# A fused attention and gated-MLP kernel whose prologue gets a new order: value tiles loaded ahead of the second weight chunk, sums of values ahead of the turns of pairs 1 and 3

## Chip, cores and metric

The kernel runs on one core of one Trainium2 chip. The metric is device microseconds of one execution; below, "us" is always that. The time before is the median of three executions.

## The reference, cut to what matters

```python
# attention: q, k, v are (4 batches, 8 heads, 768 positions, 64)
k_sum = k.reshape(B, H, 24, 32, D).max(axis=3)     # pooled keys
v_sum = v.reshape(B, H, 24, 32, D).mean(axis=3)    # pooled values
scores_l = scale * q @ k.T, kept where |i - j| < 16 (else -1e9)
scores_s = scale * q @ k_sum.T + log(32)
a = softmax(concat([scores_l, scores_s]))          # max, exp, sum, divide by sum + 1e-9
x = a @ concat([v, v_sum])                         # to 3072 tokens x 512
# MLP, weights given in float64: 512 -> 1536 -> 512
g = x @ w_gate
out = (g * sigmoid(g) * (x @ w_val)) @ w_out
```

## The kernel before, in words

The 3072 tokens are worked in six blocks of 512. The eight heads are four pairs (pair u holds heads 2u and 2u+1). The hidden width of 1536 is worked in twelve chunks j of 128. An MLP chunk is twelve products for `gate`, twelve for `val` and twelve for `down` on TensorE, each 128x128 by 128x512: every operand is split into a high and a low part, and high x high, high x low and low x high are summed, which gives the three products per 128x128 tile.

Block 0 and the weights are the prologue. Attention of block 0 goes pair by pair. `kf`, `qf` and `kq` load keys and queries. `pool(u)` takes the pooled maximum of the keys on VectorE, `sw(0,u)` and `sp(0,u)` are the score products with the window and with the pooled keys. `ttr0` and `ttr1` (four VectorE operations each, one half, that is one head of the pair, each) add the bias and take the row maximum, `exp0` and `exp1` (four ScalarE operations each) take exponentials and row sums, `rcp` inverts the sums, and `nrm` multiplies. `tr0` and `tr1` turn a half on TensorE (four 128x128 transposes), `pt0` and `pt1` copy it out of PSUM. `fv` is the matrix product that sums the values over blocks of 32, `fvc` copies the sums out. `out` and `outp` multiply the turned weights with the values (window and pooled), `split` and `rest` make the high and low part of x. `ve`, `vo` and `vr` load the three parts of the value tile.

Weights arrive as the two 32-bit halves of float64. `w_load` loads a chunk; `w_abs` (ScalarE), `w_c1`, `w_c2`, `w_s1`, `w_s2` (VectorE) rebuild float32 by integer operations, `w_hi` and `w_lo` split it into high and low part. "g", "v" and "o" are the three weights; "gv" is gate and value together, twice as wide. `silu`, `mul`, `ah` and `al` make the split activation for `down`. Steps `load`, `keys`, `scores`, `load_values`, `pool_values` and `values` belong to attention of block 1, which runs in the prologue between the chunks of block 0.

The order of the prologue is written out by hand as the text `PROLOGUE`, some 450 steps. Each step issues its instructions at once, and line 848 makes every instruction follow the one before it on the same engine. So each engine works through its own list in the order of the text, and an engine waits where its next step has an input missing, with all that stands behind it. DMAs are all issued by SyncE, in the same order. A mark behind a step picks the engine (`=a` ScalarE, `=d` VectorE, `=p` GpSimd) or the PSUM bank group (`y`, `g`: two banks each, `c`: four). A number behind a bank letter puts filler products in front of the step: `zeros` multiplies a tile of zeros, one unit for each 128 columns, with a result that is overwritten. `WARM` issues seven units at the very start.

Buffers rotate: pools `psg` and `psy` have two banks, `psc` four, tiles `a`, `ah` and `al` two buffers each, and `dec` three. `room(0)` closes the pool of block 0's attention tiles and opens the later ones in its place, so that loads behind it wait for block 0's attention to end. From block 1 on a fixed loop issues `gate`, `val` and `down` of each chunk, with attention of later blocks between them.

Of the kernel before, what the change touches and what calls it, by code (L numbers as in the profile page):

```python
# [110 lines left out]
room(0) rest(0,1) gate(0,0,0) split(0,2)=a gate(0,0,1) rest(0,2) gate(0,0,2) split(0,3)=a rest(0,3) w_c1(2,gv)
w_abs(3,gv) gate(0,0,3) gate(0,1) silu(0,0) w_c1(3,gv) w_c2(2,gv) w_s2(0,o) w_lo(0,v)=p w_s1(2,gv) w_c2(3,gv)
w_s2(2,gv) w_abs(1,o) val(0,0,0) val(0,0,1) silu(0,1) w_hi(0,o)=a val(0,0,2) w_s1(3,gv) w_c1(1,o) val(0,0,3)
load(1,0) val(0,1) w_hi(2,gv)=a w_lo(2,gv)=d w_load(2,o) w_c2(1,o) mul(0,0) ah(0,0)=a keys(1,0) gate(0,2)
w_abs(2,o) mul(0,1) w_lo(0,o)=d w_s1(1,o) al(0,0)=d ah(0,1)=a w_s2(3,gv) w_load(3,o) w_load(4,gv) silu(0,2)
scores(1,0) down(0,0) val(0,2) w_s2(1,o) w_hi(3,gv)=a al(0,1)=d ttr0(1,0) pool_values(1,0) ttr1(1,0)
w_lo(3,gv)=p w_abs(4,gv) w_abs(3,o) w_c1(4,gv) w_c1(2,o) w_c2(4,gv) gate(0,3) mul(0,2) val(0,3) w_load(5,gv)
w_s1(4,gv) w_c1(3,o) w_s2(4,gv) exp1(1,0) w_hi(1,o)=a w_c2(3,o) w_lo(1,o)=d exp0(1,0) w_hi(4,gv)=a w_s1(3,o)
w_c2(2,o) w_s2(3,o) w_s1(2,o) w_load(7,gv) w_load(6,gv) rcp(1,0) down(0,1) w_lo(4,gv)=d load(1,1) silu(0,3)
w_abs(5,gv) w_hi(3,o)=a w_c1(5,gv) mul(0,3) gate(0,4) val(0,4) ah(0,2)=a w_abs(7,gv) w_c2(5,gv) w_lo(3,o)=d  # L120
w_s1(5,gv) w_s2(2,o) nrm(1,0)=a w_hi(2,o)=a w_s2(5,gv) al(0,2)=d w_hi(5,gv)=a tr0(1,0) silu(0,4) w_abs(6,gv)
w_load(4,o) tr1(1,0) pt0(1,0)=a w_abs(4,o) w_lo(2,o)=d pt1(1,0)=a down(0,2) keys(1,1) mul(0,4) w_c1(6,gv)
w_lo(5,gv)=d w_c1(4,o) scores(1,1) ah(0,4)=a w_c2(6,gv) ah(0,3)=a ttr0(1,1) exp0(1,1) ttr1(1,1) al(0,4)=d
w_load(5,o) load_values(1,0) w_load(7,o) w_load(6,o) w_c1(7,gv) w_s1(6,gv) values(1,0)=a w_load(9,gv) gate(0,5)
al(0,3)=p w_abs(5,o) w_c2(4,o) w_s2(6,gv) w_load(8,gv) w_s1(4,o) val(0,5) w_c2(7,gv) w_hi(6,gv)=a down(0,3)
out(1,0) silu(0,5) w_lo(6,gv)=d w_s2(4,o) w_c1(5,o) w_s1(7,gv) gate(0,6) w_abs(6,o) mul(0,5) w_hi(4,o)=a
w_lo(4,o)=p down(0,4) pool_values(1,1) w_s2(7,gv) w_c2(5,o) load_values(1,1) exp1(1,1) w_c1(6,o) w_s1(5,o)
w_abs(7,o) w_abs(9,gv) w_c1(9,gv) w_c1(7,o) val(0,6) w_hi(7,gv)=a w_lo(7,gv)=d w_c2(9,gv) split(1,0)=a w_s2(5,o)
rcp(1,1) silu(0,6) w_abs(8,gv) w_c2(6,o) w_s1(9,gv) load(1,2) mul(0,6) rest(1,0) w_hi(5,o)=a w_c2(7,o) ah(0,5)=a
values(1,1)=a al(0,5)=p w_load(8,o) w_load(10,gv) w_s1(6,o) gate(0,7) silu(0,7) nrm(1,1)=a w_load(9,o) val(0,7)  # L130
w_c1(8,gv) w_lo(5,o)=d w_s2(9,gv) w_hi(9,gv)=a tr0(1,1) down(0,5) mul(0,7) ah(0,7)=a pt0(1,1)=a keys(1,2)
scores(1,2) pool_values(1,2) tr1(1,1) w_lo(9,gv)=d w_s2(6,o) w_abs(8,o) w_s1(7,o) gate(0,9) ttr0(1,2) ttr1(1,2)
pt1(1,1)=a w_c2(8,gv) out(1,1) ah(0,6)=a load(1,3) w_hi(6,o)=a w_lo(6,o)=d exp0(1,2) al(0,6)=p w_s2(7,o)
w_c1(8,o) exp1(1,2) w_hi(7,o)=a w_s1(8,gv) al(0,7)=d w_s2(8,gv) w_c2(8,o) val(0,9) down(0,6) w_lo(7,o)=d
w_abs(10,gv) w_abs(9,o) w_c1(9,o) w_hi(8,gv)=a w_c1(10,gv) w_lo(8,gv)=d down(0,7) silu(0,9) rcp(1,2) w_c2(10,gv)
w_s1(10,gv) mul(0,9) split(1,1)=a w_s2(10,gv) w_c2(9,o) nrm(1,2)=a gate(0,8) tr0(1,2) w_hi(10,gv)=a keys(1,3)
w_lo(10,gv)=d w_s1(8,o) val(0,8) ah(0,9)=a rest(1,1) room(1) w_load(11,v) w_load(11,g) silu(0,8) mul(0,8)
load_values(1,2) w_load(10,o) w_load(11,o) w_s2(8,o) pt0(1,2)=a al(0,9)=p w_abs(11,v) ah(0,8)=a w_hi(8,o)=a
w_s1(9,o) al(0,8)=d w_lo(8,o)=d gate(0,10) w_c1(11,v) tr1(1,2) pt1(1,2)=a w_c2(11,v) w_s2(9,o) w_s1(11,v)
w_s2(11,v) scores(1,3) ttr0(1,3) values(1,2)=a w_hi(9,o)=a silu(0,10) down(0,8) ttr1(1,3) val(0,10) w_abs(11,g)  # L140
w_c1(11,g) w_c2(11,g) w_lo(9,o)=p out(1,2) w_s1(11,g) w_s2(11,g) w_abs(10,o) exp1(1,3) w_hi(11,g)=d w_c1(10,o)
w_hi(11,v)=a down(0,9) w_lo(11,g)=p exp0(1,3) split(1,2)=d mul(0,10) w_lo(11,v)=d w_c2(10,o) rcp(1,3) ah(0,10)=a
rest(1,2) gate(0,11) w_abs(11,o) w_c1(11,o) w_c2(11,o) load_values(1,3) nrm(1,3)=a w_s1(10,o) tr0(1,3)
pt0(1,3)=a w_s2(10,o) al(0,10)=d w_hi(10,o)=a silu(0,11) pool_values(1,3) val(0,11) tr1(1,3) pt1(1,3)=a
values(1,3)=a w_s1(11,o) w_lo(10,o)=d down(0,10) w_s2(11,o) out(1,3) w_hi(11,o)=d w_lo(11,o)=p mul(0,11)
# [799 lines left out]
```

## Time and profile before

| what | value |
|---|---|
| time, median of 3 executions | 674.53 us (674.5 to 674.58) |
| the profiled execution's own time | 674.72 us |
| its span, first to last instruction | 673.0 us |
| TensorE matmul busy | 667.7 us, 99% of the span |
| VectorE, ScalarE, GpSimd busy | 340.0, 297.3, 139.6 us |
| share of the chain that ended last | TensorE 97%, VectorE 2% |

The span leaves out 1.7 us that lie before the first and after the last profiled instruction. A busy TensorE means that a matmul was in flight. The chain that ended last is followed back from the last instruction, at each step to what released it or to the instruction before it on its engine.

### The profile page before, as it was taken

To read this page: it belongs to the slowest core of one execution; us is meant where nothing else is said; L and a number is where in the kernel's file an instruction comes from. 1 tells how busy PE (TensorE), PEld (TensorE's weight loads), DVE (VectorE), ACT (ScalarE), POOL (GpSimd) and SP (SyncE) were. 2 spreads that over 40 slices of the span, in tenths; PEclk is the share of its full clock that TensorE was granted. 3 is DMA by queue.
4 is the path that set the end of the run, shared out by engine and by line. 5 is a ranking of instruction groups with operands and counts; after the bars stand their busy time and mean duration, and the time that the engine had idled before them with its cause. 6 is when DMAs were issued, how large, how long until landed. Compare 5 with 4: busy or idle time off the path is not lost.

```text
span 673.0 us, 12398 instructions
## 1 busy us (share of the span) xinstructions
PE 667.7 (99%) x4936; PEld 544.0 (81%) x4936; DVE 340.0 (51%) x952; ACT 297.3 (44%) x729; POOL 139.6 (21%) x137
## 2 busy tenths in 40 slices
...
GB/s 336 336 379 345 42 238 171 47 120 135 56 58 0 56 45 122 95 10 79 103 2 168 57 49 82 17 39 65 56 57 57 0 25 0 63 1 0 1 0 64
DMA packets 72059, 60.19 MB, mean 89 GB/s; under 512 B 42272, under 2 KB 60064, under 8 KB 70464
## 3 DMA queue, kind: packets, MB, share of 16 engines
...
q14 instruction: 20, 0.16, 0.1%
...
## 4 chain that ended last, share of the span: by engine, by line
PE 97%; DVE 2%; issue 0%; DVEq 0%
PE g L647 30%; PE v L647 29%; PE acc L694 29%; PE xo L612 4%; PE sc L447 2%; DVE p L505 1%; PE pp L563 1%; PE sc L458 1%; PE xo L620 1%; PE warm L740 0%; DVE ks L336 0%; PE pv L415 0%; PE sc L472 0%; PE end L694 0%; DVE m_g L219 0%
## 5 line engine op out<-in xcount | busy, mean ns | idle before, releaser
L694 PE MATMUL acc<-w_o,ah 128*128 128x512 f32 x572 | 176.2, 389 | 0.0
L647 PE MATMUL g<-xh,w_gv 128*128 128x512 f32 x480 | 159.7, 394 | 0.0
L647 PE MATMUL v<-xh,w_gv 128*128 128x512 f32 x480 | 157.9, 390 | 0.0
L658 DVE TENSOR_TENSOR a<-v,a 128x512 f32<-128x512 f32 x72 | 49.6, 689 | 199.5 <-PE v L647 197.9
L178 POOL TENSOR_TENSOR al<-a,ah 128x512 fp32r<-128x512 f32 x63 | 81.8, 1299 | 328.1 <-ACT ah L182 328.1
L694 PEld LDWEIGHTS acc<-w_o,ah 128*128 128x128 f32 x572 | 107.4, 188 | 22.2
L182 ACT CAST ah<-a 128x512 fp32r<-128x512 f32 x71 | 44.0, 621 | 168.5 <-DVE a L658 168.5
L694 PE MATMUL acc<-w_o,al 128*128 128x512 f32 x286 | 112.0, 392 | 0.0
L647 PEld LDWEIGHTS g<-xh,w_gv 128*128 128x128 f32 x480 | 90.1, 188 | 20.8 <-ACT w_o L182 0.2
L647 PEld LDWEIGHTS v<-xh,w_gv 128*128 128x128 f32 x480 | 90.1, 188 | 18.9
L653 ACT ACTIVATE a<-g 128x512 f32<-128x512 f32 x72 | 43.1, 599 | 134.8 <-PE g L647 131.8
L647 PE MATMUL g<-xl,w_gv 128*128 128x512 f32 x240 | 93.8, 391 | 0.0
L593 DVE STREAM_TRANSPOSE pt_short<-p_short 32x256 f32<-32x256 f32 x192 | 83.8, 436 | 19.8 <-POOL p_short L548 16.9
L647 PE MATMUL v<-xl,w_gv 128*128 128x512 f32 x240 | 93.4, 389 | 0.0
L694 PEld LDWEIGHTS acc<-w_o,al 128*128 128x128 f32 x286 | 53.7, 188 | 11.4 <-DVE al L178 0.2
L647 PEld LDWEIGHTS v<-xl,w_gv 128*128 128x128 f32 x240 | 45.1, 188 | 9.3
L647 PEld LDWEIGHTS g<-xl,w_gv 128*128 128x128 f32 x240 | 45.1, 188 | 8.8
L521 ACT ACTIVATE p_short<-p_short,nm 128x88 f32<-128x88 f32 x128 | 45.3, 355 | 0.2
L178 DVE TENSOR_TENSOR xl<-xo,xh 128x512 fp32r<-128x512 f32 x24 | 16.4, 686 | 56.9 <-ACT xh L182 56.8
L548 POOL TENSOR_TENSOR p_short<-p_short,ri 128x704 f32<-128x704 f32 x16 | 26.0, 1623 | 53.5 <-DVE ri L539 49.6
L647 PE MATMUL g<-xh,w_g 128*128 128x512 f32 x96 | 32.2, 396 | 0.0
L647 PE MATMUL v<-xh,w_v 128*128 128x512 f32 x96 | 31.6, 390 | 0.0
...
## 6 DMA issues: line engine op xcount, KB each, us to landing
raw_gv<-in_wgv SPq DMA_DIRECT2D x10, 1024.0 KB, 11.6
...
```

The source lines that it names most:

```text
L178: (nc.vector if e == "d" else nc.gpsimd).tensor_tensor(out=out, in0=a, in1=b.bitcast(F32), op=ALU.subtract)
L182: nc.scalar.copy(out, in_)
L447: nc.tensor.matmul(sc[h][s * SQ : (s + 1) * SQ, c * SC : (c + 1) * SC], t["q"][hs, i * SQ : (i + 1) * SQ], keys[hs], start=True, stop=True,)
L458: nc.tensor.matmul(sc[h][s * QT : (s + 1) * QT, c * KC : (c + 1) * KC], t["q"][hs, qs], t["kw"][hs, i, :], start=True, stop=True,)
L521: nc.scalar.activation(out=t["p"][:, i, :kc], in_=t["p"][:, i, :kc], func=AF.Exp, scale=-1.0, bias=t["nm"][:, i : i + 1], accum_out=t["sm" ...
L548: (nc.vector if on == "d" else nc.gpsimd).tensor_tensor(out=p, in0=p, in1=ri.rearrange("p (n o) -> p n o", o=1).broadcast_to([P, 2 * NTP, ...
L593: nc.vector.transpose(out=to[r * SQ : (r + 1) * SQ, :, s * SQ : (s + 1) * SQ], in_=t["p"][s * SQ : (s + 1) * SQ, :, at : at + SQ],)
L612: nc.tensor.matmul(ps[hs, qs], vw, t["pt"][:n, h, qs], start=k not in OWN or i == 0, stop=k not in OWN)
L647: nc.tensor.matmul(ps, w[:, cs], x, start=u == 0 and n == 0, stop=u == NP - 1 and n == 2)
L653: nc.scalar.activation(out=a, in_=A.pop(("g", k, j)), func=AF.Silu)
L658: nc.vector.tensor_tensor(out=a, in0=ps, in1=a, op=ALU.mult)
L694: nc.tensor.matmul(out, a[:, ts], w[:, cs], start=begin and n == 0, stop=end and n == 2)
```

## The change

The text of the prologue is replaced. It has the same 457 steps as before; their order, some engine marks, some bank letters and the filler numbers differ. Four places in the code change with it: the 24 columns of lead space go to chunk 11's gate weight in place of its value weight; `sp` may have filler units of its own (no step in the new text asks for any); `a_max` allocates a pair's tiles at whichever half comes first; `m_down` opens the accumulators at whichever chunk comes first.

The core of the diff, with the part of the order up to the first MLP chunk and the first steps behind it:

```diff
-kf(2) qf(2) qf(0) sw(0,2)=cc pool(2) sp(0,2) kf(0) ttr0(0,2) pool(0) exp0(0,2) ttr1(0,2) exp1(0,2)
-sw(0,0)=yg2 sp(0,0) kq(1) kq(3) ttr0(0,0) pool(1) rcp(0,2) nrm(0,2)=p ttr1(0,0) exp0(0,0) w_load(0,g)
-sw(0,1)=yg6 sp(0,1) w_load(1,gv) vr() ve() exp1(0,0) ttr0(0,1) vo() tr0(0,2)=c9 ttr1(0,1) rcp(0,0) w_abs(0,g)
-exp1(0,1) w_c1(0,g) pool(3) exp0(0,1) w_c2(0,g) w_s1(0,g) w_abs(1,gv) rcp(0,1) tr1(0,2)=g sw(0,3)=cy4 sp(0,3)
-ttr0(0,3) nrm(0,0)=p tr0(0,0)=c3 ttr1(0,3) exp0(0,3) exp1(0,3) pt0(0,2)=a w_s2(0,g) w_c1(1,gv) w_c2(1,gv)
-rcp(0,3) tr1(0,0)=y nrm(0,1)=p tr0(0,1)=y1 w_s1(1,gv) tr1(0,1)=c nrm(0,3)=d w_s2(1,gv) fv()=g pt1(0,2)=a
-w_load(0,v) out(0,2)=c pt0(0,0)=a fvc()=a outp(0,2) pt1(0,0)=a out(0,0)=c tr0(0,3)=c pt0(0,1)=a w_load(0,o)
...
+kf(2) qf(2) qf(0) sw(0,2)=cc pool(2) sp(0,2) kf(0) ttr0(0,2) exp0(0,2) ttr1(0,2) pool(0) exp1(0,2) sw(0,0)=yg5
+sp(0,0) kq(1) kq(3) ttr0(0,0) pool(1) rcp(0,2) nrm(0,2)=p ttr1(0,0) exp0(0,0) w_load(0,g) sw(0,1)=yg3 sp(0,1)
+vr() ve() exp1(0,0) ttr0(0,1) w_load(0,v) vo() w_load(1,gv) ttr1(0,1) rcp(0,0) nrm(0,0)=p pool(3) w_abs(0,g)
+sw(0,3)=cy3 sp(0,3) tr0(0,2)=c exp0(0,1) ttr1(0,3) tr1(0,2)=c w_c1(0,g) exp1(0,1) tr1(0,0)=y tr0(0,0)=y
+exp1(0,3) w_load(1,o) rcp(0,1) w_c2(0,g) ttr0(0,3) pt1(0,0)=d pt0(0,0)=a fv()=g w_abs(0,v) w_c1(0,v) pt0(0,2)=a
+w_s1(0,g) exp0(0,3) w_load(0,o) pt1(0,2)=a nrm(0,1)=p w_c2(0,v) w_s2(0,g) w_load(2,gv) rcp(0,3) fvc()=a
+w_s1(0,v) w_hi(0,g)=a cst() w_abs(1,gv) nrm(0,3)=d tr1(0,1)=c out(0,2)=y6 outp(0,2) w_s2(0,v) tr0(0,1)=c
+w_abs(1,o) tr0(0,3)=c w_lo(0,g)=d w_c1(1,gv) w_c1(1,o) tr1(0,3)=c pt0(0,1)=a out(0,0)=y w_c2(1,gv) pt1(0,3)=a
+pt0(0,3)=a w_c2(1,o) w_load(2,o) w_s1(1,gv) outp(0,0) pt1(0,1)=a out(0,1)=g w_abs(0,o) w_s1(1,o) w_s2(1,gv)
+w_c1(0,o) outp(0,1) split(0,0)=a w_abs(2,gv) split(0,2)=a out(0,3)=c outp(0,3) rest(0,0) split(0,1)=a
+w_hi(0,v)=a split(0,3)=a w_c1(2,gv) w_lo(0,v)=p rest(0,1) rest(0,2) rest(0,3) w_hi(1,gv)=a gate(0,0,0)
+w_lo(1,gv)=d gate(0,0,1) w_c2(2,gv) room(0) gate(0,0,2) w_load(3,gv) gate(0,0,3) gate(0,1) w_c2(0,o) load(1,0)
+w_s1(2,gv) w_abs(3,gv) val(0,1) val(0,0,0) w_s1(0,o) val(0,0,1) w_s2(2,gv) silu(0,0) w_c1(3,gv) keys(1,0)
+w_hi(2,gv)=a w_load(4,gv) w_load(8,o) silu(0,1) scores(1,0) val(0,0,2) w_s2(1,o) mul(0,1) w_s2(0,o)
+load_values(1,0) w_load(5,gv) w_hi(1,o)=a w_abs(4,gv) w_abs(2,o) ah(0,1)=a val(0,0,3) w_lo(2,gv)=d w_c2(3,gv)
+w_load(3,o) ttr1(1,0) mul(0,0) w_hi(0,o)=a gate(0,2) ttr0(1,0) val(0,2) exp1(1,0) w_s1(3,gv) al(0,1)=p
+w_lo(1,o)=d w_s2(3,gv) w_abs(5,gv) w_c1(5,gv) exp0(1,0) rcp(1,0) w_c1(4,gv) w_hi(3,gv)=a w_lo(3,gv)=d
+pool_values(1,0) load(1,1) down(0,1) w_lo(0,o)=p ah(0,0)=a w_load(5,o) silu(0,2) mul(0,2) gate(0,3) w_load(4,o)
...
     def w_lead(j, nm):
-        return LEAD if (nm, j) == ("v", NJ - 1) else 0
+        return LEAD if (nm, j) == ("g", NJ - 1) else 0
...
     def a_far(k, u):
+        for _ in range(int(on) if on.isdigit() else 0):
+            nc.tensor.matmul(t["sc"][0][:, NTP * KC :], warm[:, :P], warm[:, : TOK - NTP * KC], start=True, stop=True)
...
     def a_max(k, u, g):
-        if g == 0 and k >= SHORT:
+        first = "p" not in t
+        if first and k >= SHORT:
...
     def m_down(k, j):
-        if j == 0:
+        first = k not in ACC
+        if first:
```

## Rows read from the trace of the kernel before

**Rows 1.** The page: busy us, share of the span, instructions.

```profile
PE 667.7 (99%) x4936; PEld 544.0 (81%) x4936; DVE 340.0 (51%) x952; ACT 297.3 (44%) x729; POOL 139.6 (21%) x137
```

**Rows 2.** Waits of TensorE, whole span, all there are: total us, times, longest.

```profile
PE warm L740 <- DVE warm L816: 1.5, 1, 1.5
PE pp L740 <- DVE nm L505: 0.3, 1, 0.3
PE sc L484 <- DVE ks L336: 0.2, 1, 0.2
```

**Rows 3.** Windows: us, busy of PE, PEld, DVE, ACT, POOL, clock, DMA share, GB/s.

```profile
46.00:100.00 54.00, 54.00 (x356) 43.88 (x345) 53.24 (x109) 49.35 (x101) 7.60 (x8) 1.00 0.65 225
...
670.00:673.00 3.00, 0.00 (x0) 0.00 (x0) 0.32 (x1) 0.00 (x0) 0.00 (x0) 1.00 0.51 179
```

**Rows 4.** The chain that ended last: start us, us, what.

```profile
43.04 2.72 PE g L647 x12
...
46.74 2.99 PE acc L694 x12
```

**Rows 5.** Timeline of SyncE's issues: start us, us, DMA.

```profile
6.24 0.57 SPq L797 DMA_DIRECT2D vrows<-in_vO  x1
```

**Rows 6.** DMA issues to 60 us: KB each, median us to landing.

```profile
vrows<-in_vO SPq DMA_DIRECT2D x1, 1024.0 KB, 15.9
```

**Rows 7.** Timeline of TensorE: start us, us, instruction, count, idle before and releaser.

```profile
9.24 0.66 PE L484 MATMUL sc<-ks,kq 64*64 64x24 f32 x32 [0.21 <-DVE ks L336]
...
12.57 2.21 PE L740 MATMUL pp<-warm 128*128 128x512 f32 x6
14.62 1.04 PE L563 MATMUL pp<-consts,p 128*120 128x128 f32 x8
...
22.91 1.15 PE L612 MATMUL xo<-pt,vrows 96*64 96x64 f32 x32
...
25.96 0.65 PE L563 MATMUL pp<-consts,p 128*120 128x128 f32 x4
...
31.87 0.50 PE L647 MATMUL g<-xh,w_g 128*128 128x512 f32 x1
```

**Rows 8.** Timeline of VectorE, to 46 us.

```profile
7.42 0.28 DVE L505 CUSTOM_DVE_ANT_0 p<-sc,bias 128x120 f32<-128x120 f32 x1 [2.31 <-PE sc L484]
...
8.24 0.95 DVE L336 TENSOR_REDUCE ks<-kq 128x24 f32<-128x768 f32 x1
...
11.64 0.16 DVE L538 TENSOR_SCALAR sm<-sm 128x8 f32<-128x8 f32 x1
...
11.95 0.23 DVE L505 CUSTOM_DVE_ANT_0 p<-sc,bias 128x120 f32<-128x120 f32 x1
...
15.87 1.15 DVE L219 TENSOR_SCALAR m_g<-m_g 128x512 int32<-128x512 int32 x1
...
35.46 0.68 DVE L234 SCALAR_TENSOR_TENSOR m_o<-raw_o,m_o 128x512 int32<-128x512 int32 x1
36.06 1.22 DVE L227 SCALAR_TENSOR_TENSOR m_gv<-raw_gv,m_gv 128x1024 int32<-128x1024 int32 x1
37.20 0.68 DVE L219 TENSOR_SCALAR m_gv<-m_gv 128x1024 int32<-128x1024 int32 x1
```

**Rows 9.** Timeline of ScalarE, to 50 us.

```profile
10.95 0.38 ACT L521 ACTIVATE p<-p,nm 128x120 f32<-128x120 f32 x1
...
12.46 0.38 ACT L521 ACTIVATE p<-p,nm 128x120 f32<-128x120 f32 x1
...
13.97 0.66 ACT L210 ACTIVATE m_g<-raw_g 128x512 f32<-128x512 f32 x1
...
21.61 1.53 ACT L182 COPY pt<-pp 120x512 f32<-120x512 f32 x3
...
27.36 1.05 ACT L182 CAST w_gv<-m_gv 128x1024 fp32r<-128x1024 f32 x1
```

**Rows 10.** Timeline of GpSimd, to 50 us.

```profile
14.89 1.85 POOL L548 TENSOR_TENSOR p<-p,ri 128x960 f32<-128x960 f32 x1 [0.91 <-DVE ri L539]
```

More of the change, by code (lines that the diff above doesn't have):

```diff
@@ L106 @@
-rcp(0,3) tr1(0,0)=y nrm(0,1)=p tr0(0,1)=y1 w_s1(1,gv) tr1(0,1)=c nrm(0,3)=d w_s2(1,gv) fv()=g pt1(0,2)=a
-w_load(0,v) out(0,2)=c pt0(0,0)=a fvc()=a outp(0,2) pt1(0,0)=a out(0,0)=c tr0(0,3)=c pt0(0,1)=a w_load(0,o)
-w_abs(0,v) pt1(0,1)=a w_c1(0,v) w_hi(0,g)=a w_c2(0,v) w_abs(0,o) outp(0,0) tr1(0,3)=y w_lo(0,g)=d w_hi(1,gv)=a
-w_s1(0,v) w_load(2,gv) w_c1(0,o) w_s2(0,v) w_load(3,gv) w_lo(1,gv)=d w_c2(0,o) out(0,1)=y split(0,0)=a rest(0,0)
-w_s1(0,o) pt0(0,3)=a pt1(0,3)=a outp(0,1) w_abs(2,gv) split(0,1)=a w_load(1,o) cst() w_hi(0,v)=a out(0,3)=g outp(0,3)
@@ L111 @@
[L111 to L145, printed above, removed]
@@ L146 @@
-ah(0,11)=d al(0,11)=d split(1,3)=a down(0,11) rest(1,3) load(2,0)
+kf(2) qf(2) qf(0) sw(0,2)=cc pool(2) sp(0,2) kf(0) ttr0(0,2) exp0(0,2) ttr1(0,2) pool(0) exp1(0,2) sw(0,0)=yg5
+sp(0,0) kq(1) kq(3) ttr0(0,0) pool(1) rcp(0,2) nrm(0,2)=p ttr1(0,0) exp0(0,0) w_load(0,g) sw(0,1)=yg3 sp(0,1)
+vr() ve() exp1(0,0) ttr0(0,1) w_load(0,v) vo() w_load(1,gv) ttr1(0,1) rcp(0,0) nrm(0,0)=p pool(3) w_abs(0,g)
+sw(0,3)=cy3 sp(0,3) tr0(0,2)=c exp0(0,1) ttr1(0,3) tr1(0,2)=c w_c1(0,g) exp1(0,1) tr1(0,0)=y tr0(0,0)=y
@@ new lines @@
+load_values(1,0) w_load(5,gv) w_hi(1,o)=a w_abs(4,gv) w_abs(2,o) ah(0,1)=a val(0,0,3) w_lo(2,gv)=d w_c2(3,gv)
+w_load(3,o) ttr1(1,0) mul(0,0) w_hi(0,o)=a gate(0,2) ttr0(1,0) val(0,2) exp1(1,0) w_s1(3,gv) al(0,1)=p
+w_lo(1,o)=d w_s2(3,gv) w_abs(5,gv) w_c1(5,gv) exp0(1,0) rcp(1,0) w_c1(4,gv) w_hi(3,gv)=a w_lo(3,gv)=d
+pool_values(1,0) load(1,1) down(0,1) w_lo(0,o)=p ah(0,0)=a w_load(5,o) silu(0,2) mul(0,2) gate(0,3) w_load(4,o)
+nrm(1,0)=a w_c1(2,o) w_c2(4,gv) al(0,0)=p w_c2(2,o) w_abs(3,o) w_s1(4,gv) w_load(6,gv) w_s1(2,o) tr0(1,0)
@@ new lines @@
+w_c2(5,gv) w_load(7,gv) values(1,0)=a silu(0,3) keys(1,1) w_c1(3,o) w_s2(4,gv) w_load(7,o) pt0(1,0)=a
+w_load(9,o) val(0,3) w_s2(2,o) tr1(1,0) pt1(1,0)=a w_s1(5,gv) w_hi(4,gv)=a w_lo(4,gv)=d scores(1,1) ttr1(1,1)
+out(1,0) ah(0,2)=a w_hi(2,o)=a w_abs(6,gv) mul(0,3) w_abs(4,o) w_load(6,o) w_c2(3,o) w_s2(5,gv) w_s1(3,o)
+split(1,0)=a w_c1(4,o) w_c1(6,gv) w_hi(5,gv)=a down(0,0) w_s2(3,o) w_abs(7,gv) w_load(10,gv) al(0,2)=d gate(0,4)
+val(0,4) w_lo(2,o)=p silu(0,4) w_c2(6,gv) w_load(9,gv) w_lo(5,gv)=d w_s1(6,gv) pool_values(1,1) w_hi(3,o)=a
@@ new lines @@
+ttr0(1,1) mul(0,4) ah(0,3)=a down(0,2) exp1(1,1) w_s2(6,gv) w_c1(7,gv) gate(0,5) w_abs(5,o) ah(0,4)=a w_c2(4,o)
+w_abs(6,o) w_c2(7,gv) silu(0,5) w_hi(6,gv)=a al(0,3)=p val(0,5) w_abs(9,gv) w_s1(4,o) w_c1(5,o) w_lo(3,o)=p
+down(0,3) w_c2(5,o) w_s2(4,o) w_lo(6,gv)=d rest(1,0) al(0,4)=d w_hi(4,o)=a w_load(8,gv) exp0(1,1) w_s1(7,gv)
+mul(0,5) gate(0,6) w_lo(4,o)=d w_s1(5,o) ah(0,5)=a w_s2(7,gv) load_values(1,1) w_abs(8,gv) w_c1(9,gv) w_c1(8,gv)
+val(0,6) w_c1(6,o) rcp(1,1) w_hi(7,gv)=a w_lo(7,gv)=d down(0,4) w_c2(6,o) w_s2(5,o) silu(0,6) gate(0,7)
@@ new lines @@
+nrm(1,1)=a load(1,2) keys(1,2) w_c2(9,gv) w_hi(5,o)=a mul(0,6) tr0(1,1) values(1,1)=a pt0(1,1)=a al(0,5)=d
+w_s1(6,o) val(0,7) w_s1(9,gv) tr1(1,1) w_c2(8,gv) w_s2(9,gv) w_lo(5,o)=d scores(1,2) silu(0,7) w_s2(6,o)
+w_s1(8,gv) w_abs(9,o) pt1(1,1)=a mul(0,7) pool_values(1,2) w_hi(9,gv)=a out(1,1) down(0,5) ttr1(1,2) ttr0(1,2)
+w_s2(8,gv) w_load(10,o) load(1,3) w_lo(9,gv)=p ah(0,6)=a w_hi(6,o)=a w_lo(6,o)=d al(0,6)=d split(1,1)=d
+w_abs(7,o) w_abs(10,gv) w_c1(10,gv) gate(0,9) val(0,9) exp0(1,2) w_hi(8,gv)=a w_c1(9,o) w_c2(10,gv) ah(0,7)=a
@@ new lines @@
+w_c1(7,o) exp1(1,2) w_s1(10,gv) down(0,6) w_lo(8,gv)=d silu(0,9) gate(0,8) w_abs(8,o) val(0,8) rest(1,1)
+w_s2(10,gv) rcp(1,2) mul(0,9) w_hi(10,gv)=a nrm(1,2)=a load_values(1,2) tr1(1,2) al(0,7)=d silu(0,8) w_c2(7,o)
+ah(0,9)=a w_c1(8,o) w_c2(9,o) values(1,2)=a w_lo(10,gv)=d w_s1(9,o) room(1) keys(1,3) gate(0,10) w_s1(7,o)
+w_load(11,g) w_load(11,v) mul(0,8) w_s2(9,o) tr0(1,2) w_s2(7,o) w_hi(9,o)=d pt1(1,2)=a scores(1,3) w_c2(8,o)
+w_lo(9,o)=d pt0(1,2)=a out(1,2) al(0,9)=d w_abs(11,g) w_s1(8,o) silu(0,10) w_abs(11,v) load_values(1,3)
```

13 lines of the change are left out of this document (10 added, 3 removed).

## Prediction

> **What bounds the kernel.** I read the page first, then TensorE's waits, the windows, the chain that ended last, and last the four engines' lists in order of time up to the first MLP product.
>
> The page has TensorE busy for 667.7 us of a span of 673.0 [rows 1]. Its list of waits has three entries, 2.0 us in all, and the last in time is a turn's filler that waits for a row maximum of pair 3 [rows 2]. From there to the last product TensorE never stands still for as long as the list counts, and the chain that ended last runs through TensorE alone; twelve 512-wide products take 2.72 us [rows 4]. So the reader is to see two stretches. Before the first MLP product, at 31.87 us [rows 7], TensorE works on what VectorE and ScalarE give it, with fillers in between. Behind it lies one block of products, which the change reorders inside block 0 but doesn't shorten: the new text has the same steps. The end can thus move only by when the first MLP product starts, by holes in the block behind it, and by the clock, which was 1.00 [rows 3].
>
> The profiled execution took 674.72 us for its span of 673.0; its median is 674.53. I add my differences to the median.
>
> **The change, part by part.** *Code.* The lead space, the filler loop in `sp` (no step asks for it) and the two `first` flags issue no instruction: nothing.
>
> *Loads.* The values' second part landed at 6.24 + 15.9 = 22.1 us [rows 5, 6], and the first product that reads it began at 22.91 [rows 7]. It was queued behind 1024 KB of chunk 1's weights, and now behind 512 KB of chunk 0's value weight instead. By its own size and the 2.7 us that it took in this queue (an estimate: 1024 KB at some 400 GB/s), it lands 1.3 us earlier, at 20.8. Chunk 1's weights land some 7 us later, at 23; ScalarE doesn't come to them before 24.9 in the walk below, so that is free. It would cost as much as they are late beyond that.
>
> *Fillers.* Units fall from 25 to 17 (5, 3, 3 and 6). Nine took 14.62 - 12.57 = 2.05 us [rows 7], so eight are 1.8 us of TensorE. That is a gain only where TensorE's own list is the limit. The walk says it isn't, so I take 0, and keep 1.8 for the range.
>
> *Start of the order.* Up to the first row maximum at 7.42 [rows 8] nothing differs. Four maxima take 0.82 and a pooled maximum 0.87, its result after 0.95 [rows 8]. Both halves of pair 2 now come ahead of `pool(0)`: it starts at 7.42 + 1.63 = 9.05 and is done at 10.00, against 9.19. Pair 0's far scores wait for it and take 0.66 [rows 7]; their maxima start at 10.75, where before the far scores were in time. Then VectorE does 0.82 of maxima, 0.87 of `pool(1)`, 0.31 of inverse (11.64 to 11.95) [rows 8], and reaches pair 0's second half at 12.75. ScalarE gets its first value 0.3 later, at 13.05; before, that half started at 12.46 [rows 9]. From here ScalarE has something to do all the time, and its list up to pair 2's second copy is: four exponentials, the absolute value of chunk 0, twelve exponentials, a copy, an absolute value, a copy, four exponentials. Four exponentials take 12.46 - 10.95 = 1.51, an absolute value of 512 some 0.57 (0.66 less about 0.09 by which neighbours overlap, as the three copies do), a copy 0.51 [rows 9]: 5 x 1.51 + 2 x 0.57 + 2 x 0.51 = 9.71. The copy starts at 22.76 and ends at 23.34, and `out(0,2)` follows at 23.4 in place of 22.91.
>
> What hides the rest: `pool(3)` comes late (about 15.5 to 16.4), so TensorE stands still for some 2 us ahead of pair 3's far scores, but pair 3's maxima are still ready at 17.2, before ScalarE asks for them at 18.2. The sums of values now run at about 18.8 to 20.6, on data that is queued ahead of the values' second part. TensorE's list reaches `out(0,2)` at about 22.3, fillers and all, and waits 1.1 there.
>
> From `out(0,2)` to the first MLP product it was 31.87 - 22.91 = 8.96 with two turns among it. Now three turns are left, 0.44 more at most (a turn of four shows 0.65, some 0.2 of it tail) [rows 7]; they stand together and save a switch of shape. I take 0.2 (bounds 0 and 0.44): the first MLP product at 23.4 + 9.2 = 32.6, that is 0.7 later.
>
> *Behind the first product.* Chunk 1's gate comes second, and its low part is made last. ScalarE must split pair 3 (0.5), then cast chunk 1 (1.05) [rows 9], and VectorE subtracts: VectorE begins that 1.7 after the first product. From there its list runs without a gap through nine wide or integer steps to pair 1's first maxima of block 1, which free a bank for `gate(0,2)`: four wide steps at 1.14, three at 0.60, four of 512 at 0.60, the pooled keys at 0.87, an integer step of 0.3, four maxima at 0.82 [rows 8]: 1.7 + 4.56 + 1.80 + 2.40 + 0.87 + 0.30 + 0.82 = 12.45, and 0.2 for latencies. TensorE is there after 46.74 - 2.72 - 31.87 = 12.15 plus the 0.27 that a change from scores to products costs [rows 4]: 12.42. A hole of 0.25. Lower bound 0, upper bound what a VectorE 2% slower would add, 0.5.
>
> *The rest of block 0.* VectorE was busy 53.24 of 54 us there [rows 3], so cover is thin. Up to the first product it idles about 1.3 us more than before (0.8 for pair 0's scores, 0.8 for pair 3's, against some 0.3 in the same places), which the 0.7 of later start repays half: 0.6 us of its work moves behind. The margins along the new lists are some tenths; I take 0 and bound it by 0.6, and by 0.85 more for overlap of GpSimd with VectorE.
>
> That overlap has a row: a 512-wide integer step took 1.15 us at 15.87 where half of a 1024-wide one takes 0.3 [rows 8]; it ended 0.3 after GpSimd's multiply, which ran from 14.89 to 16.74 [rows 10]. The 0.85 is that loss, once. The new order gives GpSimd eight low parts in place of six. The Trainium skill ("SBUF — State Buffer", section "Who interferes with whom") says that VectorE and GpSimd share a port pair as an exclusive lock and whichever starts later waits for all of the other's instruction. The row agrees. By that rule one or two more VectorE steps would wait and the sum would be up to 0.85 higher; without it the sum stays.
>
> Sum: 0.7 + 0.25 = 0.95; 674.53 + 0.95 = 675.5 us.
>
> **The rivals.** *TensorE's list is the limit, and fillers removed are time saved.* Then the eight units go off the end: 674.53 - 1.8 = 672.7. For it: TensorE shows only 0.5 us of idle behind its first product [rows 2], and values land earlier. Against it: fillers stand where TensorE would wait anyway, and ScalarE's 9.71 us don't shrink. It decides if the second copy of pair 2 is done before 21.5.
>
> *The gain and the loss meet.* Later scores are made good, for instance by ScalarE waiting less than I think; 674.5.
>
> *Buffers are handed out in turn.* `silu(0,2)` stands ahead of `al(0,0)` and behind `al(0,1)`. If its buffer is the one that is free, no wait; if it is the older, it waits for GpSimd's low part, and the same order comes again at chunks 7 to 9. One such wait is 1.3 us and four or five make 6: 681. In the old order both rules give the same, so no row decides.
>
> *VectorE falls behind.* The 0.6 and 0.85 above, both in full: 675.5 + 1.45 = 676.95.
>
> *The clock falls in the new hole.* Some 2 us at 14.4 to 16.4 with almost nothing on TensorE. If it drops to 1.2 GHz, some 5.9 us of work ahead of `out(0,2)` (far scores, turns, sums, fillers; an estimate) take up to 11.8: +4.8 if it stays low, some 2.4 if it returns half way, 677.9. Against: at the end, 3.0 us without a product left the clock at 1.00 [rows 3]. The Trainium skill ("TensorE: Matmul & The Clock Gate", section "Part 1: The HAM clock gate (the "warmup" mystery)") says that the half clock is the default and activity lifts it, so fewer fillers count against this change; that row shows a longer hole passed without a drop.
>
> **How the numbers follow.** Forecast 0.61 (own range 674.6 to 676.6), TensorE's list 0.12, gain and loss meet 0.08, VectorE behind 0.08, buffers in turn 0.06, clock 0.05. A measurement of this kernel tells about 0.2%, 1.35 us, from no change: 673.2 to 675.9. Of the forecast 0.40 lies within and 0.21 above. Faster 0.12, same 0.48, slower 0.40. The range, 673.0 to 678.0, leaves out the first rival's core and the buffers.
>
> **What would show it.** Right: first MLP product at 32.3 to 32.8, just ahead of it a wait of about 1 us of `out(0,2)` for ScalarE's copy, a wait of about 2 us of pair 3's far scores for VectorE, the values landed by 21, and holes below 0.6 us in all behind it. Wrong: a first product before 31.5; a wait of a `gate` for a `silu` that itself waits for GpSimd; a granted clock under 1.00; or holes behind 46 us.

## The result: 679.99 us, 0.86% slower, and the profile after

The changed kernel takes 679.99 us (median of four, 679.74 to 681.54) against 674.51 of the kernel before on the same chip: ratio of the mean times 1.0086, 95% interval 1.0068 to 1.0103. The profiled execution took 679.74 us, with a span of 678.0 against 673.0 [rows 1]. The number of a line (L650) is up to four higher in the changed kernel than before; in the experiments, whose order wraps differently, it is two lower again.

TensorE's longest waits, which answer to [rows 2]: engine, what waited, for what; then us in total, times, the longest.

```profile
PE g L650 <- ACT a L656: 1.6, 1, 1.6
PE warm L744 <- DVE warm L820: 1.5, 1, 1.5
PE sc L486 <- DVE ks L336: 1.3, 3, 0.8
PE v L650 <- DVE w_v L178: 1.3, 1, 1.3
PE sc L458 <- POOL kw L184: 1.2, 1, 1.2
```

Three waits of over a microsecond are new, each happens once, and each has another releaser: ScalarE's silu, a low part by VectorE, and a copy by GpSimd. The windows say where they lie (stretch, then busy time of TensorE, its weight loads, VectorE, ScalarE and GpSimd, granted clock, DMA share, GB/s); they answer to [rows 3].

```profile
33.00:46.00 13.00, 12.83 (x83) 9.74 (x82) 12.87 (x31) 9.41 (x12) 2.41 (x5) 1.00 0.99 288
46.00:60.00 14.00, 12.42 (x57) 9.96 (x56) 12.83 (x20) 12.91 (x36) 3.15 (x4) 1.00 0.72 256
60.00:80.00 20.00, 18.81 (x139) 15.38 (x138) 19.82 (x42) 14.71 (x26) 8.60 (x5) 1.00 1.03 377
...
120.00:145.00 25.00, 23.71 (x165) 19.29 (x163) 23.20 (x53) 18.52 (x45) 6.22 (x6) 1.00 0.12 38
145.00:400.00 255.00, 255.00 (x1987) 209.47 (x1987) 124.08 (x390) 98.93 (x258) 58.46 (x53) 1.00 0.29 76
```

TensorE is short of 1.58, 1.19 and 1.29 us in three of them and full again from 145 on, at a granted clock of 1.00 throughout. TensorE's list in order of time gives the four instants that matter (start, duration, in brackets the idle time before it).

```profile
31.90 0.50 PE L650 MATMUL g<-xh,w_g 128*128 128x512 f32 x1
...
54.76 0.50 PE L650 MATMUL g<-xh,w_gv 128*128 128x512 f32 x1 [1.58 <-ACT a L656]
...
63.29 0.64 PE L458 MATMUL sc<-kw,q 64*64 64x120 f32 x16 [1.19 <-POOL kw L184]
...
138.90 0.50 PE L650 MATMUL v<-xh,w_v 128*128 128x512 f32 x1 [1.29 <-DVE w_v L178]
```

The first MLP product is where it was: 31.90 against 31.87 [rows 7]. So in this execution nothing was won or lost in front of it, and nearly the whole loss lies in the three holes. Start to start they cost 1.75 us (`gate(0,3)` begins at 54.76, `down(0,1)` began at 50.29 and needs 2.72), 1.34 (the second half of `scores(1,1)` at 63.29, the first at 61.45, a half needs 0.5) and 1.35 (`val(0,11)` at 138.90, the turns ahead of it at 137.02 need 0.53): 4.4 of the 5.0 us. (The expectations below count the first two from the last product that began ahead of them, and say 1.97 and 1.45.) Of the rest, 0.2 lies at `gate(0,1)` (34.95, behind 34.53, where a product needs 0.23) and 0.3 at `gate(0,2)` (44.75, behind 44.22).

**Hole 1, ScalarE's list.** ScalarE from the arrival of chunk 4's weights to the silu that frees the bank of `gate(0,3)`, then VectorE, then GpSimd:

```profile
42.21 1.19 ACT L210 ACTIVATE m_gv<-raw_gv 128x1024 f32<-128x1024 f32 x1 [0.87 <-DMA raw_gv<-in_wgv]
...
45.02 1.28 ACT L524 ACT_TABLE_LOAD   x1
...
48.68 1.16 ACT L210 ACTIVATE m_gv<-raw_gv 128x1024 f32<-128x1024 f32 x1 [0.74 <-DMA raw_gv<-in_wgv]
...
52.81 1.28 ACT L656 ACT_TABLE_LOAD   x1
54.11 0.60 ACT L656 ACTIVATE a<-g 128x512 f32<-128x512 f32 x1
```

```profile
46.06 2.12 DVE L227 SCALAR_TENSOR_TENSOR m_gv<-raw_gv,m_gv 128x1024 int32<-128x1024 int32 x1
```

```profile
45.80 1.30 POOL L178 TENSOR_TENSOR w_o<-m_o,w_o 128x512 fp32r<-128x512 f32 x1
...
52.87 1.79 POOL L178 TENSOR_TENSOR al<-a,ah 128x512 fp32r<-128x512 f32 x1 [5.76 <-ACT ah L182]
```

`silu(0,2)` could run from about 47.7, when `gate(0,2)` ends, but stands behind the exponentials of block 1, two table loads, and the casts and absolute values of later weights; from 42.21 to 54.11 ScalarE rests only for late weights. The VectorE step at 46.06 took 2.12 where the same form takes 1.22 elsewhere: it ended only after GpSimd's residue of the output weights. These 0.9 us didn't reach TensorE: ScalarE's next cast of a weight (51.23) waited for nothing, and VectorE itself stood 0.80 us for ScalarE's exponentials at 51.37.

**Hole 2, a copy by GpSimd.** GpSimd, and VectorE beside it:

```profile
59.96 3.27 POOL L184 COPY kw<-ks 128x96 f32<-128x96 f32 x1 [5.09 <-DVE ks L336]
```

```profile
59.82 0.42 DVE L215 TENSOR_SCALAR m_o<-m_o 128x512 f32<-128x512 f32 x1
60.15 1.22 DVE L234 SCALAR_TENSOR_TENSOR m_gv<-raw_gv,m_gv 128x1024 int32<-128x1024 int32 x1
61.29 0.68 DVE L234 SCALAR_TENSOR_TENSOR m_o<-raw_o,m_o 128x512 int32<-128x512 int32 x1
61.89 1.22 DVE L227 SCALAR_TENSOR_TENSOR m_gv<-raw_gv,m_gv 128x1024 int32<-128x1024 int32 x1
63.25 1.23 DVE L178 TENSOR_TENSOR w_gv<-m_gv,w_gv 128x1024 fp32r<-128x1024 f32 x1
```

The copy of the pooled keys takes 0.26 us alone, here 3.27. It ends at 63.23, in the first gap that VectorE leaves, 63.11 to 63.25, and TensorE's scores wait for it. Steps with two inputs in SBUF that follow one another don't always do this. A later copy of the kernel before was held for one of them only, although the next one followed at once and itself took 0.75 in place of 0.68:

```profile
114.66 1.27 POOL L184 COPY kw<-ks 128x96 f32<-128x96 f32 x1 [12.50 <-DVE ks L336]
```

```profile
114.57 1.23 DVE L178 TENSOR_TENSOR w_gv<-m_gv,w_gv 128x1024 fp32r<-128x1024 f32 x1
115.71 0.75 DVE L227 SCALAR_TENSOR_TENSOR m_o<-raw_o,m_o 128x512 int32<-128x512 int32 x1
```

Why it is three steps in one place and one in the other stays open.

**Hole 3, a low part by VectorE.** GpSimd, then VectorE:

```profile
136.93 1.37 POOL L178 TENSOR_TENSOR al<-a,ah 128x512 fp32r<-128x512 f32 x1 [3.77 <-ACT ah L182]
```

```profile
137.09 1.76 DVE L178 TENSOR_TENSOR w_v<-m_v,w_v 128x512 fp32r<-128x512 f32 x1
```

GpSimd began 0.16 earlier, VectorE's step took 1.76 in place of 0.68 and ended 0.55 after GpSimd's: the price of a step that finds GpSimd ahead of it is about what is left of GpSimd's (1.08 us lost, 1.21 left). Which of the two comes first hangs on little: in e3, e5 and e9 below, where the same residue is still GpSimd's, VectorE began 0.16 to 0.18 us ahead of it, its step took 0.68 or 0.69, and TensorE didn't wait.

### The profile page after: what moved, and what is told of

It reads as the page before. It is cut to its first block, busy times and chain, and to the rows that moved or that the text cites. A ratio compares the mean times of both kernels' runs of the same rounds, so it can differ in the third digit from the quotient of the medians.

```text
span 678.0 us, 12395 instructions
## 1 busy us (share of the span) xinstructions
PE 666.8 (98%) x4930; PEld 543.3 (80%) x4930; DVE 341.9 (50%) x953; ACT 296.1 (44%) x726; POOL 146.1 (22%) x139
## 4 chain that ended last, share of the span: by engine, by line
PE 92%; ACT 2%; issue 2%; DVE 2%; POOL 1%; POOLq 0%; DVEq 0%
PE g L650 28%; PE v L650 28%; PE acc L697 28%; PE xo L615 4%; PE sc L447 2%; ACT p L524 2%; PE pp L566 1%; PE sc L458 1%; PE xo L623 1%; POOL kw L184 1%; PE warm L744 0%; DVE p L508 0%; DVE ks L336 0%; DVE w_v L178 0%; PE end L697 0%
## 5 line engine op out<-in xcount | busy, mean ns | idle before, releaser
L650 PE MATMUL g<-xh,w_gv 128*128 128x512 f32 x480 | 159.6, 393 | 1.8 <-ACT a L656 1.6
L650 PE MATMUL v<-xh,w_gv 128*128 128x512 f32 x480 | 157.9, 390 | 0.0
L650 PEld LDWEIGHTS g<-xh,w_gv 128*128 128x128 f32 x480 | 90.1, 188 | 23.4 <-ACT a L656 2.0
L650 PEld LDWEIGHTS v<-xh,w_gv 128*128 128x128 f32 x480 | 90.1, 188 | 18.9
L650 PE MATMUL g<-xl,w_gv 128*128 128x512 f32 x240 | 93.8, 391 | 0.0
L650 PE MATMUL v<-xl,w_gv 128*128 128x512 f32 x240 | 93.4, 389 | 0.0
L650 PEld LDWEIGHTS v<-xl,w_gv 128*128 128x128 f32 x240 | 45.1, 188 | 9.3
L650 PEld LDWEIGHTS g<-xl,w_gv 128*128 128x128 f32 x240 | 45.1, 188 | 8.9
L184 POOL COPY kw<-ks 128x384 f32<-128x384 f32 (+2 forms) x28 | 16.6, 591 | 82.0 <-DVE ks L336 55.6
L650 PE MATMUL v<-xh,w_v 128*128 128x512 f32 x96 | 31.9, 392 | 1.3 <-DVE w_v L178 1.3
```

The source lines that it names most:

```text
L184: (nc.vector if e == "d" else nc.gpsimd).tensor_copy(out, in_)
L650: nc.tensor.matmul(ps, w[:, cs], x, start=u == 0 and n == 0, stop=u == NP - 1 and n == 2)
```

## The experiments

The kernel before ran beside them: 674.65 us for e1 to e4, 674.01 for e5 to e8, 674.08 for e9 to e11, 674.18 for e12.

**The halves.** The new order up to the first MLP product with the old order behind it, and the reverse; all code of the change stays but for the lead space, which goes with the old rest.

```diff
 e1: steps ahead of gate(0,0,0) as in the new text, then the old text's remaining steps
 e2: steps ahead of gate(0,0,0) as in the old text, then the new text's remaining steps
```

> The new order up to the first MLP product, behind it the old order of what is then left. Theory (the loss sits behind the first product, in three holes that the new order of the rest makes): holes of 1 us and more are gone, the time is that of the kernel before within 0.7 us, 674.2 to 675.2. Rival (the new front leaves VectorE behind by some 1.3 us of idle time and the rest only shows it): 676 or more, with holes behind 46 us in the old rest too.

Measured 676.89, ratio 1.0034 (1.0022 to 1.0047). The number is the rival's, the trace is neither's: in the profiled execution the first product comes at 31.54, TensorE stands 0.15 to 0.2 us at two gate products, and its last product ends only 0.4 us later than before's. The other 1.2 of the 1.6 us by which the span is longer lie behind it, where the last store landed late:

```profile
out<-o_end SPq DMA_DIRECT2D x1, 96.0 KB, 2.9
```

(issue to landing; before and after show 1.6). It was 2.8 in e7 below, the other kernel with this order, and 1.6 or 1.7 in every further one. That belongs to neither theory, and I have no cause for it.

> The old order up to the first MLP product, behind it the new order of what is then left. Theory (the loss sits in the rest): 678.5 to 681, with holes at the gate of chunk 3, at block 1's scores of pair 1 and at the value product of chunk 11. Rival (the new front is what makes VectorE late): below 677.

Measured 680.85, ratio 1.0097 (1.0082 to 1.0112): by its number what the theory says. By the trace, two of the three holes come with the new rest: that at the scores (0.8; the copy takes 3.27 us again) and that at the value product of chunk 11 (1.3). The hole at the gate of chunk 3 isn't there, and the two largest lie at the seam, where front and rest now don't fit:

```profile
36.01 0.51 PE L648 MATMUL g<-xl,w_g 128*128 128x512 f32 x1 [1.94 <-DVE xl L176]
...
48.07 0.47 PE L648 MATMUL g<-xh,w_gv 128*128 128x512 f32 x1 [1.25 <-DVE nm L506]
```

So the halves cost 2.2 and 6.2 us against 5.5 for the whole, and they don't add up.

**Holes 2 and 3 by themselves.**

```diff
 e3, in a_keys:
-                "p",
+                "d" if (k, u) == (1, 1) and pos == 0 else "p",
 e4, in the order:
-al(0,10)=p
+al(0,10)=d
```

> The changed kernel with one GpSimd copy, that of the pooled keys of pair 1 of block 1 (3.27 us in the profile where its like takes 0.26), made by VectorE. Theory (GpSimd's copy waits for three VectorE operations with two inputs in SBUF that follow each other, and the scores wait for it): the hole of 1.2 us at those scores goes, the copy takes under 0.3 us, time 678.6 to 679.1. Rival (VectorE's list is late there whoever copies): the hole stays or moves, 679.7 to 680.2.

Measured 677.84, ratio 1.0047 (1.0032 to 1.0062): 2.15 us back, more than expected. Hole 2 is gone, and hole 3 too: what follows is displaced, and the low part there took 0.69 with GpSimd's residue beginning 0.17 after it. The median span fell by more, from 678.3 to 675.55, which is about the price of both holes; 2.1 to 2.9 us of each execution lie outside the span here, 1.7 in the change, and I have no cause for that.

> The changed kernel with the low part of the activation of chunk 10 made by VectorE in place of GpSimd. Theory (VectorE's subtraction for chunk 11's value weight takes 1.76 us in place of 0.68 because GpSimd's subtraction holds the way): it takes 0.7 us, the hole of 1.3 us at the value product of chunk 11 shrinks to 0.3 or less, time 678.7 to 679.2. Rival (that subtraction is late by its own inputs and would end when it does): hole within 0.3 us of 1.3, time 679.7 to 680.2.

Measured 679.25, ratio 1.0064 (1.0049 to 1.0079): 0.74 back, just above the upper end. The low part takes 0.68, and TensorE's wait for it falls from 1.3 to 0.3. The median span fell by 1.55, from 678.3 to 676.75: one of the four executions has 3.5 us outside its span in place of 1.7.

**Hole 1 by one transfer, and all three.**

```diff
 e5: w_load(8,o) from ahead of load_values(1,0) to behind w_load(4,o)
 e6: e3, e4 and e5 together
```

> The changed kernel, with chunk 8's output weights sent for behind those of chunk 4 instead of ahead of chunk 5's gate weights. Theory (the first hole, 1.97 us, is ScalarE's list, held up by weights that land late behind a transfer that nothing needs yet): chunk 5's gate weights land some 2 us earlier (46.6 in place of 48.59), ScalarE's wait of 0.74 us for them goes, the hole shrinks to 1.0 to 1.3, and the time is 679.0 to 679.4 us. Rival (the hole is VectorE's and GpSimd's, through the blocked step on chunk 3's weights at 46.06): hole and time stay, 679.8 to 680.2.

Measured 677.64, ratio 1.0057 (1.004 to 1.0073), against 674.01 here. The number is below the theory's, but not for its reason, and the theory falls in this form: chunk 5's weights landed 1.6 us earlier and ScalarE no longer waited for them, but chunk 4's landed at 42.96, 0.8 later, and the silu still began at 54.07. The first hole is shorter (a wait of 1.00) because the first product came later in that execution (32.44), and hole 3 didn't form.

> The changed kernel with all three mends together: the pooled keys' copy of pair 1 on VectorE, the last residue of chunk 10 on VectorE, chunk 8's output weights later. Theory (three separate holes, each with its own cause): the gains add, 676.0 to 677.0 us, and what is left over the kernel before is the front's share. Rival (a hole that is closed opens again further on, because VectorE has no slack left): 677.8 or more, no better than the copy alone.

Measured 676.78, ratio 1.0044 (1.0029 to 1.0058). The time is the theory's, the trace half the rival's: holes 2 and 3 are gone, the first has grown to 2.09. ScalarE waited there for chunk 4's weights until 43.52, 1.3 later than in the change, and then had no rest until its silu at 54.52. Two VectorE steps were stretched by GpSimd too, 2.21 and 1.78 in place of 1.22 and 0.68, but ScalarE waited for neither.

**The front again.**

```diff
 e7: e1 with five fillers ahead of pair 3's far scores
-sp(0,3)
+sp(0,3)=5
 e8: the old order with
-w_load(1,gv) vr() ve() exp1(0,0) ttr0(0,1) vo()
+vr() ve() exp1(0,0) ttr0(0,1) w_load(0,v) vo() w_load(1,gv)
 and fv() ahead of tr0(0,1)
```

> The new order up to the first MLP product with the old order behind it, as in the run of the new front alone (676.89), with five filler products put ahead of pair 3's far scores, into the stretch of 14.4 to 16.4 us in which TensorE stands. Theory (the new front costs time because TensorE stands there, through the clock in some executions): 674.5 to 675.5 us and a mean clock of 1.000 in every run. Rival (the cost is in when the weights and values land, whatever TensorE does meanwhile): 676.4 to 677.4.

Measured 676.12, ratio 1.0041 (1.0027 to 1.0056), between the two. The profiled execution is the slowest of seven, 679.74, the others lie at 675.94 to 676.85; its windows show why:

```profile
10.00:16.00 6.00, 4.80 (x132) 3.27 (x132) 5.23 (x38) 5.46 (x27) 2.16 (x2) 1.00 1.02 398
16.00:24.00 8.00, 8.00 (x107) 7.28 (x104) 4.29 (x24) 5.65 (x25) 3.21 (x2) 0.58 1.03 417
```

The granted clock is 0.58 from 16 to 24 us, mostly the lower level of 1.2 GHz, behind a stretch in which TensorE stood for 1.2 us of six. The price is 3.6 us against the median; 3.1 of it show at the first product, which follows the first row maximum by 28.2 us in place of 25.1. The fillers stood behind the first hole, not in it, so what they would do there is not shown.

> The kernel before with only the two edits that the change is named for: the value tiles are loaded ahead of chunk 1's weights, and the sums of the values go ahead of the turns of pairs 1 and 3; all else in the old order. Theory (these two are free, the new order of the rest costs the time): 674.2 to 675.2 us. Rival (chunk 1's weights land too late for the first gate, or the sums wait for the values and hold up the turns): 675.6 or more, with a hole at the second gate product.

Measured 682.33, ratio 1.0125 (1.011 to 1.014): 8.3 us more than the kernel before (674.01). That is the rival's side, but not its place: no gate waits, `out(0,2)` does. TensorE and ScalarE:

```profile
28.71 1.60 PE L610 MATMUL xo<-pt,vrows 96*64 96x64 f32 x18 [6.04 <-ACT pt L180]
```

```profile
24.06 1.12 ACT L208 ACTIVATE m_gv<-raw_gv 128x1024 f32<-128x1024 f32 x1 [6.31 <-DMA raw_gv<-in_wgv]
```

In the old text `w_abs(1,gv)` comes early on ScalarE; its weights, behind the value tiles and chunk 0's value weight, now land at 24.0, and the exponentials of pair 3 and the copies of pair 2 stand behind it. Part of the price is the clock: it was 0.63 from 24 to 33 us, and 18 of the window products take 1.60 us in the line above where 32 take 1.15 [rows 7]. So the loads are free only with the new order of ScalarE's steps.

**Where the copy stands.**

```diff
 e9:
-pool_values(1,0) load(1,1) ... values(1,0)=a silu(0,3) keys(1,1)
+load(1,1) keys(1,1) pool_values(1,0) ... values(1,0)=a silu(0,3)
 e11, the kernel before:
-mul(0,4) w_c1(6,gv) w_lo(5,gv)=d w_c1(4,o)
+w_c1(6,gv) w_lo(5,gv)=d w_c1(4,o) mul(0,4)
```

> The changed kernel, with the pooling of pair 1's keys for block 1 moved ahead of the pooling of pair 0's values on VectorE (and its load with it), so that the pooled keys' copy, still on GpSimd, falls beside a reduction in place of three steps with two inputs. Theory (GpSimd's 3.27 us copy is held off by VectorE's steps, and by the kind of step that runs beside it): the copy takes 0.3 to 0.7 us, the second hole of 1.45 us goes, and the time is 677.4 to 678.4 us, as with the copy on VectorE. Rival (the copy on GpSimd is late or slow for another reason, its place in the queue or its operands): it stays above 2 us and the time at 679.5 or more.

Measured 676.42, ratio 1.0037 (1.0023 to 1.0052), against 674.08: the theory, and 1 us better. GpSimd, and VectorE beside it:

```profile
53.79 0.27 POOL L182 COPY kw<-ks 128x96 f32<-128x96 f32 x1 [8.03 <-DVE ks L334]
```

```profile
53.65 0.94 DVE L354 TENSOR_REDUCE vr<-vt 128x24 f32<-128x768 f32 x1
```

The same copy on the same engine takes 0.27 beside a reduction, and TensorE doesn't wait. What held it off was VectorE's work beside it. Hole 3 didn't form either, which is some 1.35 of the 3.6 us that came back.

> The kernel before, with one VectorE step moved: chunk 4's product, whose one input lies in PSUM and beside which the pooled keys' copy ran in 0.27 us, goes behind the three steps that followed it, so that the copy meets steps whose inputs all lie in SBUF. Theory (such steps hold GpSimd off as long as they follow one another): the copy takes 1.9 to 2.5 us in place of 0.27, TensorE waits 0.2 to 0.6 us for it at the scores of pair 1, and the time is 674.2 to 674.8 against 674.0. Rival (a copy on GpSimd is held for one step at most): the copy takes under 1.2 us and TensorE does not wait.

Measured 675.11, ratio 1.0015 (1.0006 to 1.0025), and the expectation was missed: the copy took 0.27 again, because the step that now followed waited 0.62 us for ScalarE and left VectorE idle just then.

```profile
68.57 0.69 DVE L213 TENSOR_SCALAR m_gv<-m_gv 128x1024 f32<-128x1024 f32 x1 [0.62 <-ACT m_gv L208]
```

So this run says nothing of either theory. The product itself came 3 us later, and TensorE's next gate 0.37 later, counted from the first product (71.38 behind 32.16, in the trace before 70.72 behind 31.87); that is part of the 1.0 us that it cost.

**Hole 1 by four moves, and the sum.**

```diff
 e10: load_values(1,0) to behind w_load(3,o), w_load(8,o) to behind w_load(4,o), both of which
 come behind w_load(5,gv); w_lo(0,o)=p to behind al(0,0)=p
-ah(0,0)=a
+ah(0,0)=p
 e12: e9; load_values(1,0) and w_load(8,o) as in e10
-al(0,10)=p
+al(0,10)=d
```

> The changed kernel with four moves for the first hole: chunk 8's output weights and pair 0's values for block 1 are sent for behind chunk 5's gate weights; GpSimd's residue of chunk 0's output weights goes behind that of chunk 0's gated sums; the rounding of chunk 0's gated sums goes from ScalarE to GpSimd. Theory (ScalarE's list has no idle time from the landing of chunk 4's gate weights at 42.13 to the silu at 54.11 but for waits on transfers, and VectorE is blocked for 0.9 us by that residue): the silu starts 1.2 to 1.6 us earlier, the first hole shrinks from 1.97 to 0.4 to 0.8, and the time is 678.4 to 678.9. Rival (the shorter first hole is given back at the later ones, because VectorE is what falls behind): 679.5 to 680.2.

Measured 681.23, ratio 1.0112 (1.0091 to 1.0133): the rival, and worse. ScalarE had no wait for chunk 5's weights, but GpSimd's two residues now ran at 46.4 to 50.3, beside VectorE's steps for chunk 3, of which one took 2.31 in place of 1.22; ScalarE's cast waited 1.09 for it. The copy then met four two-input steps in a row and took 4.41:

```profile
60.09 4.41 POOL L182 COPY kw<-ks 128x96 f32<-128x96 f32 x1 [8.55 <-DVE ks L334]
```

TensorE waited 2.8 for it, and then the clock fell in the profiled execution:

```profile
64.00:70.70 6.70, 6.15 (x56) 5.06 (x57) 5.37 (x16) 4.31 (x5) 1.72 (x2) 0.50 1.02 422
```

> The changed kernel with the keys' pooling of pair 1 early as in that run (676.42), chunk 8's output weights and pair 0's values for block 1 sent for behind chunk 5's gate weights, and the residue of chunk 10's gated sums on VectorE; GpSimd's work at the first hole stays where it is. Theory (the second and third hole are GpSimd held off by VectorE or VectorE by GpSimd, the first is ScalarE's list with two waits for late weights, 1.02 and 0.37 us there): the second and third hole stay shut, the first shrinks from 1.3 to 0.4 to 0.8, and the time is 675.2 to 676.0 us against 674.1, the rest over the kernel before being two short holes of 0.15 to 0.25 us at the gate products behind the first and the front. Rival (VectorE has no slack, so each hole that is shut opens another): 676.4 or more.

Measured 675.62, ratio 1.0025 (1.0016 to 1.0035), against 674.18: the theory. TensorE's waits behind the front are one:

```profile
PE g L648 <- ACT a L654: 0.5, 1, 0.5
```

`silu(0,2)` begins at 52.92, 1.2 earlier than in the changed kernel, and holes 2 and 3 are shut. Four moved steps and one given to VectorE give back 4.0 of the 5.5 us. None of these versions beats the kernel before.

## Why the prediction was wrong, by its own steps

The forecast was 675.5 us, with 673.0 to 678.0 as the range; measured were 679.99.

- *Loads.* Right. The values landed at 21.1 (20.8 forecast), chunk 1's weights at 23.6 (23), and nobody waited for either. The run of the two named edits shows that this hangs on ScalarE's new order.
- *Start of the order.* Right in mechanism, and hidden in this execution. The two stand-stills are there:

```profile
15.80 0.66 PE L486 MATMUL sc<-ks,kq 64*64 64x24 f32 x32 [0.82 <-DVE ks L336]
...
22.70 1.09 PE L615 MATMUL xo<-pt,vrows 96*64 96x64 f32 x29 [0.41 <-ACT pt L182]
```

  They are 0.82 for pair 3's pooled maximum and 0.41 of `out(0,2)` for the copy, against some 2 and 1.1. The first row maximum began at 6.79, where I took 7.42 from before. In nine profiled executions with this front and an undisturbed clock ahead of the first product, that product follows the first maximum by 25.1 to 25.2 us (31.48 behind 6.37, 32.51 behind 7.39) and in one of them by 25.4; before's by 24.45. The term of 0.7 is that difference. But old fronts vary too: e11's first product follows by 24.8, e2's by 25.8. And the nine first products lie at 31.9 on average, since an earlier maximum is passed on in full, while e2's and e11's, with first maxima at 6.34 and 7.33, were at 32.17 and 32.16. So the term was about right for a start like before's (0.3 to 0.6 between e3 and e5, with 7.39 and 7.34, and the old fronts with 7.42 and 7.33), and about nothing over several.
- *Behind the first product.* Right. A hole of 0.25 at `gate(0,2)` was forecast, for VectorE's first maxima of block 1. They ended at 44.60, and 0.3 stood there, start to start:

```profile
44.22 0.40 PE L650 MATMUL v<-xh,w_v 128*128 128x512 f32 x1
44.75 0.47 PE L650 MATMUL g<-xh,w_gv 128*128 128x512 f32 x1
```

  The 0.2 at `gate(0,1)`, for chunk 1's low part (done at 34.81), was not forecast.
- *The rest of block 0* is the step that failed: "The margins along the new lists are some tenths; I take 0 and bound it by 0.6, and by 0.85 more for overlap". It was 4.4 in three places. I walked the lists up to `gate(0,2)` and took the rest as a total, VectorE's work against its time. But the first hole, 1.75, comes from ScalarE's list, which I had not walked, and in which `silu(0,2)` stands late. That this list sets the hole is shown by e12, where its waits for weights are shorter, the silu comes 1.2 earlier and TensorE's wait falls from 1.58 to 0.46; that the place of that one step is to blame is argued, since no run moved it. And the overlap of GpSimd with VectorE, which I priced as one loss of 0.85 from [rows 8, 10], was neither one nor bounded by a step. A VectorE step stretched by 1.1 made the third hole (1.35), and the copy, which VectorE held off for 3.0, the second (1.34); a stretch of 0.9 had no effect. The 0.85 was also read too high: a 512-wide integer step takes 0.42 by itself (at 74.89 in the trace before), so the row's 1.15 shows a loss of 0.73.
- *The skill's rule.* The Trainium skill ("SBUF — State Buffer", section "Who interferes with whom") was the warning, and the forecast gave it 0.85. The trace agrees that the later engine waits (2.12 and 1.76 in place of 1.22 and 0.68), and, with that page, that a reduction beside a GpSimd copy leaves it alone (0.27). It differs in length: the rule has the loser wait for one instruction, as the copy at 114.66 of the kernel before did; the copy of the second hole waited for three and, in another run, four.
- *Rivals.* "VectorE falls behind" named the right pair of engines, with 1.45 where it cost more. "Buffers are handed out in turn" is out: `silu(0,2)` began at 54.11 while GpSimd's residue of chunk 0 ran from 52.87 to 54.66. "TensorE's list is the limit" and "the gain and the loss meet" are out by the waits. "The clock falls in the new hole" didn't happen in the profiled execution of the change (1.00 in every window), but did in one with the same front and five fillers more (e7), at 3.6 us where 2.4 to 4.8 were forecast. Of the other three executions of the change, that of 681.54 us has a mean clock of 0.998. The row held against this rival, 3.0 us without a product at the end, didn't decide: in e10 the clock fell behind a hole of 2.8.

Open: the 1.4 us that the last version is still over the kernel before (its trace shows a wait of 0.5 and, start to start, 0.2 and 0.3 us at `gate(0,1)` and `gate(0,2)`), the late last store of the two kernels with the new front alone, and how often the clock falls in the new front. That VectorE's work holds the copy off was shown twice, by giving the copy to VectorE and by moving it beside a reduction; making the old order slower by it was tried and missed, and for how many steps a copy is held isn't explained.
